# One attention-plus-two-block kernel: sums of weight columns formed once and kept in DRAM, output products in groups of two, GpSimd taken out of the second block

## The chip, the cores and the metric

One Trainium2 chip, one of its cores. The metric is the device time of the program in microseconds (us); lower is better. Engines are named as in the profile: PE is TensorE's matmul, PEld its weight load, DVE is VectorE, ACT is ScalarE, POOL is GpSimd, SP is SyncE (here it only issues DMAs).

## What is computed

Attention with a threshold mask (4 batches, 8 heads, 576 rows, 64 columns), whose output is reshaped to 2304 x 512, and then two feed-forward blocks. Only the second block bears on the change:

```python
x = _moe_ref(x, w_in, w_out, alpha)   # first block, d_ff = 2048
a = x @ w1                            # second block: 512 -> 1024
b = x @ w2
h = a * b @ w3                        # 1024 -> 1024
return h @ w_out                      # 1024 -> 512
```

All weights arrive as float64 (int64 words for the kernel) and are converted on the chip. Every matmul factor is cut in a high and a low part (`split_hi`, `split_lo`), and a product is three passes: high by high, high by low, low by high.

## The kernel before, in words

**Stages.** Attention runs to about 300 us of the trace. The first block follows, tile by tile in the order 0, 4, 1, 2, 3 (tile 4 holds 256 rows, the others 512). Then a stage multiplies w3 by the second w_out (`wp_job`), to about 757 us. Then the second block runs to 1052 us; it multiplies x by w1 and w2, multiplies the two results element by element, and multiplies that by the product of w3 and w_out.

**Order.** From the first block on, every instruction is an `Op` with a list of engines and an assumed cost on each. `list_order` (line 34) plays through these costs and fixes both the engine and the order in which each engine gets its instructions; on the chip each engine runs its list in that order and waits where a semaphore is not there yet. An op that lists "P" and "V" goes to POOL or DVE, whichever the planner expects to be earlier. `slots` gives how many buffers each tag has. PE's order in the second block is fixed by the order in which the code makes the ops (`pe`, line 1300).

**Second block.** 24 iterations: three passes (two halves of 384 rows each) by eight slices `f` of 128 columns. In an iteration `a` and `b` of both halves come from seven products of six 384-column matmuls each, instead of eight (a Strassen-Winograd scheme). The products J(1) to J(7) need sums and differences on three sides:

- of x, per pass: four differences (`difference`, tag `tt`, line 1170) and seven split tiles (tag `T`), in `moving`;
- of the weights, per iteration: four sums of 128 x 256 (line 1241, all on POOL), and four split tiles (tag `sw`, line 1262), in `stationary`. These tiles are made two iterations ahead;
- of the results: an ACT copy of the first two products (`c1`, `c11`, line 1380) and five DVE additions from PSUM (`u2`, `v5`, `c22`, `c12`, `c21`, line 1375).

Then `ab1` and `ab0` multiply a by b for either half (line 1375 too, as `ct<-ct`), ACT and DVE split the result (`x<-ct`, lines 183 and 188), and six output products `d` of three 512-column matmuls each (line 930 in this stage) are put in a queue that the next iteration empties, one `d` after each of six products (`d_next`). The products use two PSUM banks in turn, so a product waits until the bank's old value has been read: J(2) for `c1`, J(5) for `u2`, J(7) for `c11`, J(3) for `v5`, J(4) for `c22`, and the next iteration's first two for `c12` and `c21`. In the last iteration no `d` stands between the products.

**Where the weights come from.** While the first block runs, `put_by` loads slices of the later weights, converts them (`weight`: ACT, then three DVE steps, then a rounding add on POOL, line 218), and stores them in DRAM. `turns` says beside which step of the first block each conversion is planned: w1 and w2 first, then w_out, and w3 (which PE also transposes) during tile 2. In the second block `stationary` loads one slice of each of w1 and w2 per iteration.

Of the kernel before, what the change touches and what calls it, by code (L numbers as in the profile page):

```python
# [10 lines left out]
F32 = mybir.dt.float32  # L11
# [109 lines left out]
def kernel(  # L121
# [99 lines left out]
    with tc.manual_schedule():  # L221
# [565 lines left out]
        def weight(src, prio, after=()):  # L787
# [19 lines left out]
            ld = op({"S": 0.65}, load, prio - 12, take="raw")  # L807
# [41 lines left out]
        scratch = {}  # L849

        def put_by(key, src, prio, after, turned=False):
# [21 lines left out]

            s_ = op({"S": 0.65}, store, prio + (9 if turned else 4), [a])
# [4 lines left out]
        stored = {}  # L879

# [13 lines left out]
        def split(n, src, dst, prio, deps, take, free=(), psum=False):  # L894
            h = op(
                {"A": part(n, 0.48 if psum else 0.52)},
                lambda e: split_hi(ENG[e], dst()[:, 0, 0:n], src()),
                prio,
                deps,
                take=take,  # L900
            )
            l = op(
                {"V": part(n, 0.66 if psum else 0.6)},
                lambda e: split_lo(ENG[e], dst()[:, 1, 0:n], src(), dst()[:, 0, 0:n]),
                prio + 0.3,
                [h],
                free=free,
            )
            return h, l
# [149 lines left out]
        turns += [(t, f) for t in (1, 2) for f in sorted([3, 7, 11] + list(range(1, 14)))]  # L1059
# [95 lines left out]
        def moving(p, prio, deps_by_slot):  # L1155
# [11 lines left out]
            def temp():  # L1167
                return lazily(lambda: blk["pool"].tile([128, 2 * HT], F32, tag="tt", name="tt", bufs=3))

            def difference(dst, a, b, prio, deps):  # L1170
# [17 lines left out]
                return op({"P": 1.9, "V": 0.95}, emit, prio, deps, take="tt")  # L1188
# [15 lines left out]
            for i, (name, src, row, made) in enumerate(sources):  # L1204
# [11 lines left out]
                h = op({"A": 0.9}, lambda e, f=emit: f(e, False), prio + 1 + 0.5 * i, [made] if made else deps, take="T")  # L1216
                l = op({"V": 0.95, "P": 1.9}, lambda e, f=emit: f(e, True), prio + 1.3 + 0.5 * i, [h], free=[made] if made else [])
# [5 lines left out]
        def stationary(f, prio):  # L1223

            boxes, loads = [], []
            for i in range(2):
                x = lazily(lambda: dn.tile([128, 512], F32, tag="m", name="w12", bufs=3))

                def load(e, x=x, i=i):
                    nc.sync.dma_start(out=x(), in_=scratch[i, f])  # L1230

                boxes.append(x)
                loads.append(op({"S": 0.65}, load, prio - 8 + 0.1 * i, [stored[i, f]], take="m"))
            a, b = boxes
            sums = lazily(lambda: dn.tile([128, 1024], F32, tag="raw", name="sums"))
            lo2, hi2 = slice(0, 256), slice(256, 512)

            def tt(dst, x, y, how, prio, deps, take=None):
                o = op(
                    {"P": 0.74},  # L1240
                    lambda e: ENG[e].tensor_tensor(out=dst(), in0=x(), in1=y(), op=how),
                    prio, deps, take=take,
                )
                for d in deps:
                    if d in loads:
                        o.wait[d] = 2.6
                return o

            s1 = tt(lambda: sums()[:, lo2], lambda: b()[:, lo2], lambda: b()[:, hi2], ALU.add, prio - 3, [loads[1]], "raw")
            s3 = tt(lambda: b()[:, lo2], lambda: a()[:, lo2], lambda: b()[:, lo2], ALU.subtract, prio - 2.5, [s1, loads[0]])  # L1250
            s2 = tt(lambda: sums()[:, hi2], lambda: sums()[:, lo2], lambda: a()[:, lo2], ALU.subtract, prio - 2, [s1, loads[0]])
            s4 = tt(
                lambda: sums()[:, 512:768], lambda: a()[:, hi2], lambda: sums()[:, hi2], ALU.subtract, prio - 1.5, [s2]
            )
            parts, made = [], []
            for i, (src, deps, n, frees) in enumerate((
                (lambda: a(), [loads[0]], 512, [loads[0]]),
                (lambda: sums()[:, 0:512], [s1, s2], 512, []),
                (lambda: b(), [s3], 512, [loads[1]]),
                (lambda: sums()[:, 512:768], [s4], 256, [s1]),  # L1260
# [3 lines left out]
                    {"A": part(n, 0.52)}, lambda e, w=w, src=src, n=n: split_hi(ENG[e], w()[:, 0, 0:n], src()),  # L1264
                    prio + 0.5 * i, deps, take="wu0",
                )
                l = op(
                    {"P": part(n, 1.25), "V": part(n, 0.6)},
                    lambda e, w=w, src=src, n=n: split_lo(ENG[e], w()[:, 1, 0:n], src(), w()[:, 0, 0:n]),
                    prio + 0.5 * i + 0.3, [h], free=frees,  # L1270
                )
                for d in deps:
                    if d in loads:
                        h.wait[d] = 2.6
# [3 lines left out]
            for o in (s4,):  # L1278
                o.free.append(loads[0])
                loads[0].left += 1  # L1280
            made[1][1].free.append(s1)
            s1.left += 1
            s3.free.append(loads[0])
            loads[0].left += 1
# [212 lines left out]
```

## Time and profile before

| | us |
|---|---|
| median of three runs | 1058.74 (1057.98 to 1059.26) |
| the profiled execution | 1059.3 |
| its span, first to last instruction | 1057.5 |
| PE busy | 1021.9 (97%) |
| DVE busy | 767.4 (73%) |
| ACT busy | 575.9 (54%) |
| POOL busy | 486.5 (46%) |

A busy time adds up the recorded durations of an engine's instructions. Matmuls are pipelined, so a PE that is busy all the time is not necessarily at its best rate, and a wait of some tenths of a us shows as a gap between two of them. The time of an instruction on DVE or POOL as recorded includes any time in which it had begun and could not go on. Windows are counted in us from the first instruction.

### The profile page before, as it was taken

Reading aid. Unit: us, or ns where it says so; the run is one execution under the profiler, and the core shown is the slowest. Engines: PE = TensorE matmul, PEld = TensorE weight load, DVE = VectorE, ACT = ScalarE, POOL = GpSimd, SP = SyncE. Lnnn points to the kernel's source line nnn. Section 1 sums busy time; section 2 is a strip of 40 time slices with the busy share of each in tenths; the row PEclk is TensorE's granted clock in tenths of the full one; section 3 lists DMA queues with packets and bytes.
Section 4 is the critical chain, followed back from the end, with each engine's and each line's share of the span. In section 5 each row is a group of like instructions: output and inputs, shape, how many; then the busy total and the mean of one; then the engine's idle time right before and its main releaser. Section 6 shows DMA issues by size and latency. Waiting matters only on the chain.

```text
span 1057.5 us, 16956 instructions
## 1 busy us (share of the span) xinstructions
PE 1021.9 (97%) x5870; PEld 866.9 (82%) x5870; DVE 767.4 (73%) x1483; ACT 575.9 (54%) x1115; POOL 486.5 (46%) x609
## 2 busy tenths in 40 slices
PE   8999999999989999999999999999999989999997
PEld 6777787777758889988888888887888889888887
DVE  7999999999858886565566644358476796678663
ACT  5999989898866655545454432232333442344332
POOL 4888888888632332132212300024573463455320
PEclk9999999999999999999999999999999999999999
DMA  5353534344113333345534511103211121113101
GB/s 132 83 148 90 146 91 134 103 122 116 37 60 103 117 120 121 120 150 163 165 99 153 167 51 43 38 31 90 80 50 50 41 100 50 41 41 100 50 11 60
DMA packets 66837, 96.92 MB, mean 92 GB/s; under 512 B 14400, under 2 KB 43072, under 8 KB 66752
## 3 DMA queue, kind: packets, MB, share of 16 engines
q1 hardware_dynamic: 64544, 95.84, 30.6%
q8 instruction: 46, 0.75, 0.3%
q10 hardware_dynamic: 2208, 0.01, 0.1%
q14 instruction: 39, 0.32, 0.1%
HBM read 70.79 MB, written 15.20 MB: 81 GB/s over the span
## 4 chain that ended last, share of the span: by engine, by line
PE 79%; DVE 9%; POOL 5%; issue 3%; ACT 2%; DMA 1%; POOLq 0%; DVEq 0%; ACTq 0%
PE h L930 23%; PE acc L930 21%; PE h L1311 13%; PE pv_ps L518 8%; PE s_ps L402 5%; PE pt_ps L491 5%; DVE ct L1375 4%; POOL p L474 3%; PE tr L291 2%; DVE x L188 2%; POOL ks L181 1%; DVE tt L1184 1%; DVE T L188 1%; ACT ct L1380 1%; POOL qs L181 1%
## 5 line engine op out<-in xcount | busy, mean ns | idle before, releaser
L930 PE MATMUL h<-x,wa 128*128 128x512 f32 (+1 forms) x960 | 212.1, 370 | 1.2 <-ACT x L183 1.1
L1311 PE MATMUL h<-T,sw 128*128 128x384 f32 x1008 | 202.6, 341 | 9.8 <-DVE ct L1375 5.1
L930 PE MATMUL acc<-gs,wu 128*128 128x512 f32 (+1 forms) x960 | 209.6, 368 | 0.4 <-DVE wu L829 0.4
L1311 PEld LDWEIGHTS h<-T,sw 128*128 128x128 f32 x1008 | 179.9, 189 | 29.0 <-ACT ct L1380 11.3
L930 PEld LDWEIGHTS h<-x,wa 128*128 128x128 f32 x960 | 167.2, 189 | 32.2 <-ACT x L183 2.7
L930 PEld LDWEIGHTS acc<-gs,wu 128*128 128x128 f32 x960 | 168.2, 189 | 30.8 <-DVE wu L829 0.8
L218 POOL TENSOR_TENSOR m<-m,raw 128x512 int32<-128x512 int32 x58 | 81.4, 1403 | 230.2 <-DVE m L213 189.3
L426 DVE TENSOR_REDUCE sm<-s_ps 128x1 f32<-128x576 f32 x144 | 105.6, 752 | 12.9 <-PE s_ps L402 12.8
L437 ACT ACTIVATE e<-s_ps,sm 128x576 f32<-128x576 f32 x144 | 106.1, 765 | 7.4 <-DVE sm L426 4.7
L474 POOL TENSOR_SCALAR p<-p,sm 128x576 f32<-128x576 f32 x128 | 97.4, 767 | 27.1 <-DVE sm L467 18.1
L1375 DVE TENSOR_TENSOR ct<-h,ct 128x384 f32<-128x384 f32 x120 | 66.6, 555 | 50.7 <-PE h L1311 49.9
L451 DVE SCALAR_TENSOR_TENSOR p<-s_ps,sm,e 128x576 f32<-128x576 f32 x128 | 102.7, 812 | 0.9 <-ACT e L437 0.9
L1006 DVE SCALAR_TENSOR_TENSOR g<-h,salpha_sb,g 128x512 f32<-128x512 f32 (+1 forms) x80 | 55.6, 695 | 58.1 <-ACT g L1001 57.6
L491 PE MATMUL pt_ps<-ident,p 128*128 128x128 f32 x576 | 86.0, 276 | 11.6 <-ACT pt L505 8.8
L183 ACT CAST gs<-g 128x512 fp32r<-128x512 f32 (+1 forms) x80 | 46.3, 578 | 90.1 <-PE acc L930 71.9
L1001 ACT ACTIVATE g<-h,sign_sb 128x512 f32<-128x512 f32 (+1 forms) x80 | 51.3, 642 | 74.1 <-PE h L930 66.8
L183 ACT CAST x<-ct 128x384 fp32r<-128x384 f32 x48 | 24.7, 515 | 118.0 <-DVE ct L1375 117.9
L491 PEld LDWEIGHTS pt_ps<-ident,p 128*128 128x128 f32 x576 | 64.6, 140 | 26.7 <-POOL praw L474 10.4
L518 PE MATMUL pv_ps<-pt,vraw 128*64 128x256 f32 (+1 forms) x640 | 84.7, 411 | 0.4 <-ACT xT L531 0.2
L188 DVE TENSOR_TENSOR gs<-g,gs 128x512 fp32r<-128x512 f32 (+1 forms) x80 | 58.9, 737 | 34.0 <-ACT gs L183 33.5
L505 ACT COPY pt<-pt_ps 128x512 f32<-128x512 f32 x128 | 74.5, 597 | 15.6 <-PE pt_ps L491 14.6
L930 PE MATMUL acc<-wp,x 128*128 128x512 f32 x288 | 81.9, 395 | 0.3 <-DVE x L188 0.3
(127 smaller groups left out, 1709.4 us busy)
## 6 DMA issues: line engine op xcount, KB each, us to landing
raw<-in_moe_w_dram SPq DMA_DIRECT2D x32, 512.0 KB, 3.9
raw<-in_moe_w_out_dram SPq DMA_DIRECT2D x24, 512.0 KB, 3.5
w<-w SPq DMA_DIRECT2D x48, 256.0 KB, 2.6
qU<-qT SPq DMA_DIRECT2D x30, 320.0 KB, 4.1
wraw<-in_moe_w_in_dram SPq DMA_DIRECT2D x14, 512.0 KB, 3.7
w<-m SPq DMA_DIRECT2D x24, 256.0 KB, 2.2
z<-w SPq DMA_DIRECT2D x24, 256.0 KB, 2.7
qraw<-in_q_dram SPq DMA_DIRECT2D x16, 256.0 KB, 4.0
```

What stands on the lines that cost most here:

```text
L188: eng.tensor_tensor(out=dst, in0=src, in1=hi.bitcast(F32), op=ALU.subtract)
L218: nc.gpsimd.tensor_tensor(out=mc[0], in0=mc[0], in1=mc[1], op=ALU.add)
L426: nc.vector.tensor_reduce(out=sm_of(u, 0), in_=st[u], axis=AX.XY, op=ALU.max, negate=True)
L437: nc.scalar.activation(out=es[u].rearrange("p (j s) -> p j s", j=2), in_=st[u], func=AF.Exp, bias=sm_of(u, 0))
L451: nc.vector.scalar_tensor_tensor(out=p_at(u).rearrange("p (j s) -> p j s", j=2), in0=st.pop(u), scalar=sm_of(u, 1), in1=es.pop(u).rearrang ...
L474: nc.gpsimd.tensor_scalar(out=out, in0=in_, scalar1=sm_of(u, 3), scalar2=1.0, op0=ALU.mult, op1=ALU.mult)
L491: nc.tensor.transpose(t[:, i, :], p[:, at + i * 128 : at + (i + 1) * 128], ident)
L505: nc.scalar.copy(out=pt[:, g, 0:4, to], in_=ps)
L518: nc.tensor.matmul(out=o[64 * hh : 64 * hh + 64, 0:n], lhsT=vr[:, hh, i, :], rhs=pt[:, 0 if i == 4 and not half else hh, i, :], start=(i = ...
L930: nc.tensor.matmul(out=out, lhsT=l, rhs=r, start=first and i == 0, stop=last and i == n - 1)
L1311: nc.tensor.matmul(out=bank_()[:, 0:HT], lhsT=w()[:, ap_, kc * 128 : kc * 128 + 128], rhs=x()[:, bp, kc * HT : kc * HT + HT], start=first ...
L1375: lambda e: ENG[e].tensor_tensor(out=dst(), in0=x(), in1=y(), op=how),
```

## The change

- **Weight sums.** The four sums per slice move from `stationary` (POOL, 24 times four) to `put_sums`, called when w2's slice has been converted beside the first block (DVE, eight times four). Three tensors per slice are stored instead of two: w1's slice, the changed slice of w2, and the 768-column sums. `stationary` loads these three.
- **Order of conversions.** w_out now comes first, then w3 (tile 1 instead of tile 2), then w1 and w2 (tile 2 and the beginning of tile 3).
- **Engines.** In the second block all that could go to POOL or DVE goes to DVE: the differences, the low parts of `T` and `sw`, and the multiplications `ab0` and `ab1`. The planner's costs are new.
- **Output products.** Of the six `d`, two stand after J(6), two after J(5), one after J(3), one after J(4); before, one stood after each of J(6), J(2), J(5), J(7), J(3), J(4). In the last iteration four of them stand between the products.
- **Buffers.** `tt` has four buffers instead of three, `ct` six of 384 columns instead of eight (several results overwrite their inputs).
- **Stores.** The two 64-row stores of a tail group are one store.

```diff
@@ put_by @@
+            if key[0] == 1:
+                f = key[1]
+                made_12[key] = box, a
+                box_a, box_b, sums, s3, s4 = put_sums(f, prio + 4)
+                held = [first, first_of.pop((0, f)), box["ld"]]
...
+                    ("a", 512, lambda: box_a["x"], s4),
+                    ("b", 512, lambda: box_b["x"], s3),
+                    ("s", 768, lambda: sums()[:, 0:768], s4),
...
+                    outs.append(op({"S": 0.65}, put, prio + 6, [dep]))
+                o = op({"D": 0.0}, lambda e: None, prio + 6, outs, free=held)
...
+        def put_sums(f, prio):
...
+                return op(
+                    {"V": 0.43},
+                    lambda e: ENG[e].tensor_tensor(out=dst(), in0=x(), in1=y(), op=how),
+                    prio, deps,
+                )
+
+            A = lambda half: lambda: x_of(box_a)[:, half]
+            Bb = lambda half: lambda: x_of(box_b)[:, half]
+            s1 = tt(lambda: sums()[:, lo2], Bb(lo2), Bb(hi2), ALU.add, prio, [a, b])
+            s3 = tt(Bb(lo2), A(lo2), Bb(lo2), ALU.subtract, prio + 0.2, [s1])
+            s2 = tt(lambda: sums()[:, hi2], lambda: sums()[:, lo2], A(lo2), ALU.subtract, prio + 0.4, [s1])
+            s4 = tt(lambda: sums()[:, 512:768], A(hi2), lambda: sums()[:, hi2], ALU.subtract, prio + 0.6, [s2])
@@ the order of the conversions @@
-        later = [((i, f), cols(w, f)) for f in range(NF2) for i, w in enumerate((w1, w2))]
-        later += [(("o", j), rows(w_out2, j)) for j in range(NF2)]
+        later = [(("o", j), rows(w_out2, j)) for j in range(NF2)]
         later += [(("3", i, h), rows(w3, i, h)) for i in range(NF2) for h in range(2)]
+        later += [((i, f), cols(w, f)) for f in range(NF2) for i, w in enumerate((w1, w2))]
...
-        turns += [(t, f) for t in (1, 2) for f in sorted([3, 7, 11] + list(range(1, 14)))]
+        turns += [(1, f) for f in sorted([3, 7, 11] + list(range(1, 14)))]
+        turns += [(2 + f // NF, f % NF) for i in range(NF2) for f in (3 * i, 3 * i + 1)]
@@ moving @@
-                return op({"P": 1.9, "V": 0.95}, emit, prio, deps, take="tt")
+                o = op({"V": 1.0}, emit, prio, deps, take="tt")
+                o.bias = 0.3
+                return o
...
-                l = op({"V": 0.95, "P": 1.9}, lambda e, f=emit: f(e, True), prio + 1.3 + 0.5 * i, [h], free=[made] if made else [])
+                l = op({"V": 1.0}, lambda e, f=emit: f(e, True), prio + 1.3 + 0.5 * i, [h], free=[made] if made else [])
@@ stationary @@
-            for i in range(2):
+            for i, (what, n) in enumerate((("a", 512), ("s", 768), ("b", 512))):
...
-            s1 = tt(lambda: sums()[:, lo2], lambda: b()[:, lo2], lambda: b()[:, hi2], ALU.add, prio - 3, [loads[1]], "raw")
...
-                    {"P": part(n, 1.25), "V": part(n, 0.6)},
+                    {"V": 0.158 + n / 960},
                     lambda e, w=w, src=src, n=n: split_lo(ENG[e], w()[:, 1, 0:n], src(), w()[:, 0, 0:n]),
@@ the iteration @@
-            P_ = part(HT, 0.66)
+            P_ = 0.56
             q = now
-            n_d = 0 if end else 1
             j1 = J(1, bx, True, x_free, q)
...
-            d_next(q + 2.1, n_d)
+            d_next(q + 2.1, 2)
...
-            d_next(q + 3.8, n_d)
...
-            d_next(q + 5.5, n_d)
+            d_next(q + 5.5, 2)
...
-            d_next(q + 7.3, n_d)
...
-            d_next(q + 9.0, n_d)
+            d_next(q + 9.0, 1 if not end else 0)
...
-            d_next(q + 10.7, 99 if end else 1)
+            d_next(q + 10.7, 1 if not end else 99)
...
-            both = {"V": part(HT, 0.6), "P": part(HT, 1.25)}
-            ab1 = tt(t["c12"], t["c12"], t["c22"], ALU.mult, 0, q + 10.2, [c12, c22], free=[c22], engines=both)
-            ab0 = tt(t["c21"], t["c11"], t["c21"], ALU.mult, 0, q + 11.8, [c21, c11], free=[c11], engines=both)
+            ab1 = tt(t["c12"], t["c12"], t["v"], ALU.mult, 0.56, q + 9.7, [c12, c22], free=[v5])
+            ab0 = tt(t["u"], t["c11"], t["u"], ALU.mult, 0.56, q + 11.4, [c21, c11], free=[c11])
...
-                            for k_ in range(2):
-                                r0 = (2 * c + k_) * S + SM
-                                nc.sync.dma_start(out=out[r0 : r0 + ST, :], in_=out_()[64 * k_ : 64 * k_ + 64])
+                            dst = out.rearrange("(b s) d -> b s d", b=B)[2 * c : 2 * c + 2, SM:S, :]
+                            nc.sync.dma_start(out=dst, in_=out_())
...
-        slots = {"raw": 2, "m": 3, "u": 2, "gs": 2, "x": 4, "h": 4, "acc": 1, "wa": 16, "wu0": 8, "wu1": 8, "ct": 8, "tt": 3, "T": 7}
+        slots = {"raw": 2, "m": 3, "u": 2, "gs": 2, "x": 4, "h": 4, "acc": 1, "wa": 16, "wu0": 8, "wu1": 8, "ct": 6, "tt": 4, "T": 7}
```

## Rows read from the trace of the kernel before

**Rows 1.** Windows, tile 3 and second block: PE, PEld, DVE, ACT, POOL busy, clock, DMA
```profile
594.00:677.00 83.00, 83.00 (x377) 68.79 (x376) 41.72 (x68) 27.02 (x44) 5.78 (x4) 1.00 0.23 67
...
757.00:1052.20 295.20, 285.07 (x1442) 258.17 (x1440) 203.97 (x299) 111.24 (x225) 136.76 (x133) 0.99 0.17 52
```

**Rows 2.** What the seven products' matmuls and weight loads (line 1311) waited for: us, times
```profile
  ACT ct L1380: 16.0, 29
  DVE ct L1375: 11.6, 7
```

**Rows 3.** Chain of work that ended last, second block: start us, us, what
```profile
1022.98 1.06 PE h L1311 x6
1024.04 0.70 PE acc L930 x3
1024.74 2.10 PE h L1311 x12
...
1044.65 1.38 PE h L930 x6
```

**Rows 4.** Busy time by windows (columns of rows 1), each from one iteration's J(2) to a later one's
```profile
791.22:840.02 48.80, 47.47 (x242) 42.82 (x241) 31.90 (x50) 15.48 (x33) 19.29 (x20) 1.00 0.17 45
840.02:868.26 28.24, 25.38 (x120) 22.86 (x121) 26.55 (x34) 16.32 (x29) 20.62 (x16) 0.94 0.26 91
868.26:940.88 72.62, 70.76 (x361) 64.15 (x360) 47.97 (x74) 23.20 (x49) 28.70 (x30) 1.00 0.16 45
940.88:955.11 14.23, 11.99 (x60) 10.84 (x61) 13.22 (x20) 9.53 (x20) 9.92 (x9) 1.00 0.12 36
955.11:1027.38 72.27, 70.75 (x362) 64.25 (x361) 50.20 (x76) 25.98 (x53) 29.52 (x29) 1.00 0.19 59
```

**Rows 5.** Timeline, end of one iteration: start us, us, engine, instruction [idle before]
```profile
815.68 1.31 PE L1311 MATMUL h<-T,sw 128*128 128x384 f32 x6 [0.42 <-ACT ct L1380]
...
813.06 1.64 DVE L1375 TENSOR_TENSOR ct<-ct 128x384 f32<-128x384 f32 x1
814.62 0.42 DVE L188 TENSOR_TENSOR sw<-sums,sw 128x256 fp32r<-128x256 f32 x1
...
814.73 0.51 ACT L183 CAST x<-ct 128x384 fp32r<-128x384 f32 x1 [2.05 <-DVE ct L1375]
815.15 0.47 ACT L1380 COPY ct<-h 128x384 f32<-128x384 f32 x1
...
812.69 1.60 POOL L188 TENSOR_TENSOR sw<-w,sw 128x512 fp32r<-128x512 f32 x1
```

**Rows 6.** Timeline, the iteration after: one DVE and two POOL instructions
```profile
822.90 0.56 DVE L1375 TENSOR_TENSOR ct<-ct 128x384 f32<-128x384 f32 x1
...
822.28 0.74 POOL L1241 TENSOR_TENSOR w<-w,w 128x256 f32<-128x256 f32 x1
822.98 1.08 POOL L1241 TENSOR_TENSOR sums<-sums,w 128x256 f32<-128x256 f32 x1
```

**Rows 7.** Groups of instructions by line and shape, 757 to 1052.2 us
```profile
L1375 DVE TENSOR_TENSOR ct<-h,ct 128x384 f32<-128x384 f32 x120 | 66.6, 555 | 50.7 <-PE h L1311 49.9
L1375 DVE TENSOR_TENSOR ct<-ct 128x384 f32<-128x384 f32 x46 | 46.6, 1013 | 1.0
L188 DVE TENSOR_TENSOR T<-xT,T 128x768 fp32r<-128x768 f32 x2 | 1.9, 952 | 0.1
```

**Rows 8.** Instructions that touch the weight tiles: duration ns min/median/max, first, last start
```profile
L188 DVE TENSOR_TENSOR sw<-w,sw x29: 679/693/1777, 753.2 to 1026.2; 128x512 fp32r<-128x512 f32 x29
```

**Rows 9.** Timeline where a pass begins: a DVE difference, and a stall of PE
```profile
849.11 1.49 DVE L1184 TENSOR_TENSOR tt<-xT,tt 128x768 f32<-128x768 f32 x1
...
856.78 2.29 PE L1311 MATMUL h<-T,sw 128*128 128x384 f32 x6 [1.89 <-DVE ct L1375]
```

**Rows 10.** Timeline, issues of the half-size stores at the end
```profile
1050.09 2.44 SPq L1451 DMA_DIRECT2D out_dram<-o  x4
```

**Rows 11.** Costliest groups of instructions over the whole span (page): the rounding adds
```profile
L218 POOL TENSOR_TENSOR m<-m,raw 128x512 int32<-128x512 int32 x58 | 81.4, 1403 | 230.2 <-DVE m L213 189.3
```

More of the change, by code (lines that the diff above doesn't have):

```diff
@@ L805, in add @@
                 box["x"] = cvt_round((box["m"], box["c"]))
-            ld = op({"S": 0.65}, load, prio - 12, take="raw")
+            ld = box["ld"] = op({"S": 0.65}, load, prio - 12, take="raw")
             c = op({"A": 0.57}, low, prio, [ld] + after)
@@ L1167, in temp @@
             def temp():
-                return lazily(lambda: blk["pool"].tile([128, 2 * HT], F32, tag="tt", name="tt", bufs=3))
+                return lazily(lambda: blk["pool"].tile([128, 2 * HT], F32, tag="tt", name="tt", bufs=4))
             def difference(dst, a, b, prio, deps):
@@ L1250, in stationary, with load @@
[L1250 to L1254, printed above, removed]
-            parts, made = [], []
[L1256 to L1260, printed above, removed]
+            for i, (what, n) in enumerate((("a", 512), ("s", 768), ("b", 512))):
+                tag = "raw" if n > 512 else "m"
+                x = lazily(lambda n=n, tag=tag: dn.tile([128, 1024 if n > 512 else n], F32, tag=tag, name="w12", bufs=3 if tag == "m" else 2))
+                def load(e, x=x, what=what, n=n):
+                    nc.sync.dma_start(out=x()[:, 0:n], in_=scratch[what, f])
+                boxes.append(x)
+                loads.append(op({"S": 0.65}, load, prio - 8 + 0.1 * i, [stored["12", f]], take=tag))
@@ L1261, in stationary @@
+            a, sums, b = boxes
+            parts, made = [], []
+            for i, (src, ld, n, last) in enumerate((
+                (lambda: a(), loads[0], 512, True),
+                (lambda: sums()[:, 0:512], loads[1], 512, False),
+                (lambda: sums()[:, 512:768], loads[1], 256, True),
+                (lambda: b(), loads[2], 512, True),
             )):
@@ L1277, in stationary @@
                 made.append((h, l))
[L1278 to L1284, printed above, removed]
             def at(i, half):
                 return (lambda: parts[i]()[:, :, 256 * half : 256 * half + 256]), made[i]
-            return {1: at(0, 0), 2: at(0, 1), 3: at(3, 0), 4: at(2, 1), 5: at(1, 0), 6: at(1, 1), 7: at(2, 0)}, made
+            return {1: at(0, 0), 2: at(0, 1), 3: at(2, 0), 4: at(3, 1), 5: at(1, 0), 6: at(1, 1), 7: at(3, 0)}, made
         x_bank, y_bank = bank("h"), bank("h")
@@ L1321, in temp @@
         def temp():
-            return lazily(lambda: blk["pool"].tile([128, HT], F32, tag="ct", name="ct", bufs=8))
+            return lazily(lambda: blk["pool"].tile([128, HT], F32, tag="ct", name="ct", bufs=6))
         def d_piece(g, gs, f, first, last):
@@ L1359 @@
             made = S_made.pop(i)
-            t = {n: temp() for n in ("c1", "u2", "v5", "c11", "c22", "c12", "c21")}
+            t = {n: temp() for n in ("u", "v", "c11", "c12")}
             def J(k, bank_, first, deps, prio, s=s, m=m):
@@ L1401 @@
+            j5 = J(5, by, True, [u2], q + 4.5)
+            v5 = tt(t["v"], Y, t["u"], ALU.add, P_, q + 5.8, [j5, u2], take="ct")
+            d_next(q + 5.5, 2)
+            j7 = J(7, bx, True, [c11], q + 6.9)
+            c22 = tt(t["v"], X, t["v"], ALU.add, P_, q + 8.0, [j7, v5])
             j3 = J(3, by, False, [v5], q + 8.0)
-            c12 = tt(t["c12"], Y, t["u2"], ALU.add, P_, q + 9.3, [j3, u2], take="ct")
-            d_next(q + 9.0, n_d)
+            c12 = tt(t["c12"], Y, t["u"], ALU.add, P_, q + 9.1, [j3, u2], take="ct")
```

84 lines of the change are left out of this document (43 added, 41 removed).

## Prediction

> **What bounds the kernel now.** I read the busy windows first. From the first block's tile 3 on, PE has no gap: 83.00 of 83.00 us [rows 1]. In the second block it is busy 285.07 of 295.20 us, with DVE at 203.97 and POOL at 136.76 [rows 1]. So only the second block has something to give back, and the question is what PE waits for there. The waits of the products' line name ACT's copies out of PSUM (16.0 us in 29 waits, weight loads included) and DVE's additions (11.6 us in 7) [rows 2].
>
> Next comes the length of an iteration. The chain of waits gives the price of work without a stall: two products in a row 2.10 us, a lone product 1.06, a lone output product `d` 0.70 [rows 3]. The present pattern is one pair of products, five lone ones and six lone `d`: 2.10 + 5 x 1.06 + 6 x 0.70 = 11.60 us. The windows show what the iterations take [rows 4]: 48.80 us for four, 72.62 and 72.27 for six each, that is 2.40 + 3.02 + 2.67 = 8.1 us over the floor in 16 steady iterations (0.5 each). Where a new pass begins they show 28.24 us for two and 14.23 for one, 5.0 + 2.6 = 7.7 us over. Both together are 15.8 us.
>
> The steady stall has one cause, which the timeline shows [rows 5]. POOL begins a low part of `sw` at 812.69 and holds on for 1.60 us. DVE begins `ab0` at 813.06 and takes 1.64 us, ending at 814.70, when POOL has been done for about 0.4 us. The same multiplication took 0.56 us ten us later [rows 6], when POOL's own instruction, begun just after it, took 1.08 instead of 0.74 us: the two don't run together, the second waits. ACT has `x<-ct` at the head of its list, waiting for `ab0`; behind it stands the copy `c1`, at 815.15; and J(2), which waits for `c1`, starts 0.42 us late [rows 5]. Over the block the multiplications average 1013 ns, against 555 for the additions that read PSUM, which POOL does not disturb [rows 7].
>
> **The change, part by part.**
>
> *GpSimd out of the second block.* All of its 136.76 us of work go [rows 1]; the sums disappear, the rest comes to DVE. DVE's load then, at undisturbed durations: 120 additions at 0.555 (66.6 us), 48 multiplications and 48 low parts of x at 0.56 (53.8), 72 low parts of `sw` at 0.69 (49.7) [rows 6 to 8], 24 half-width ones at 0.42 (10.1) [rows 5], 14 low parts of `T` at 0.95 (13.3) [rows 7], eight differences at as much (7.6): 201 us, as now (203.97), because the lengthening goes. A steady iteration needs 7.5 of 11.5 us. `ab0` becomes 1.08 us shorter, more than the stall of 0.42, so the steady stall goes. What is late next is judged below. The 8.1 us are the gain; I keep back 0.1 us an iteration, 2.0 in all, for an urgent DVE instruction behind one of 0.56 to 0.95 us (bounds 0 and the present 8.1).
>
> *Groups of two.* The new pattern is three pairs of products (6.30), one lone (1.06), two pairs of `d` at 1.38 (2.76), two lone `d` (1.40): 11.52 us [rows 3]. That is 0.08 less, and over some 22 iterations 1.8 us. It moves covers too. J(2) gets 0.68 us more behind J(1), so this edit alone would also hide the 0.42 us stall. J(4) loses 0.70: between J(7) and J(4) stand J(3) and one `d`, 1.06 + 0.70 = 1.76 us, in which `c22` must run. It needs 0.56 and some 0.2 for two hops; an instruction of 0.95 in front of it still fits (1.71), two don't. The other covers stay as they are. In the last iteration four `d` move up between the products, and two are left to hide the chain `c12`, `ab1`, split high, split low (four times about 0.55, with hops 2.8 us) after J(3), against 1.06 + 1.38 = 2.44: I charge 0.5 us (bounds 0 and 1.5).
>
> *Beginning of a pass.* Here DVE is the engine that is late: it is busy 26.55 of 28.24 us [rows 4], and PE's stalls end with DVE additions (1.89 us before J(5), the longest) while differences run on DVE too, one of them for 1.49 us where a `T` of the same size takes 0.95 [rows 9, 7]. After the stall the products' group took 2.29 us instead of 1.06 [rows 9, 3], and the window's granted clock is 0.94, where the steady ones have 1.00 [rows 4]: part of the time ran at the lower of PE's two levels, 1.2 GHz instead of 2.4, and that part (1.2 us on this group alone) goes with the stall. With POOL's share on DVE, the two iterations need 2 x 7.5 + 7 x 0.95 + up to five differences (4.8) = 26.5 us, less 0.08 us of overlap between neighbours (814.62 starts before 813.06 + 1.64 [rows 5]) for some 40 instructions: 23.3 us, against 23.0 of PE. There is no margin if all differences fall there; with a fourth `tt` buffer the last difference of a pass need not wait for the pass before, and without any differences it is 18.9. So I keep back 2.0 us here and 0.5 at the second beginning, 2.5 of 7.7 (bounds 0 and 7.7).
>
> *Sums in the first block.* DVE gets 32 additions of 0.42 us, 13.4 us, in tile 2 and the beginning of tile 3; half-width, as the row taken for the price [rows 5]. They lie beside a PE without gaps, with DVE at 41.72 of 83 us in tile 3 [rows 1]; the bounds are 0 and 13.4, a gain is excluded since PE has nothing to give back there, and I take 0. New is the wait of the first sum on POOL's rounding add (1.40 us [rows 11]): behind it on DVE stand `prelu` and `split_lo` of the current step, and PE's `x2_job` waits for these; it is planned two and a half steps later, so several us are covered. The three steps of reordering (w_out, w3, then w1 and w2) move the same conversions; w3's transposes go to tile 1. The slots of tag `m` and `raw` are held until the stores have landed; the next pair is planned two steps on. SP issues 8 stores and 24 loads more on a queue that has no other work near its limit (DMA share 0.17 [rows 1]), and the `sw` tiles are made two iterations ahead: 0.
>
> *Stores at the end.* Two issues fewer of 0.61 us [rows 10] stand ahead of the last stores: 0.5 us (bounds 0 and 1.2).
>
> **Sum.** Gains 8.1 + 7.7 + 1.8 + 0.5 = 18.1 us; kept back 2.0 + 2.5 + 0.5 = 5.0; net 13.1. The profiled execution took 1059.3 us (span 1057.5, 1.8 around it), which gives 1046.2; against the median 1058.74 it is 1045.6 us. With nothing kept back it is 1040.6.
>
> **A rule on sharing work.** DVE is busy 69% of the second block and 94% of the windows where a pass begins [rows 1, 4]; that is the one fact that speaks against loading it. The Trainium skill, "Perfetto Trace Analysis", section "Optimizing Scalar/DVE Operations", says that with DVE saturated it may make sense to offload work even to GpSimd, though offloading between the two might not help since they share an SBUF read port. By the first half of that rule the change goes the wrong way, which is the rival A below; the pair of rows with 0.56 and 1.08 us is on the side of its second half.
>
> **The rivals.**
>
> *A. DVE becomes the bound where a pass begins.* All eleven `T` and `tt` instructions of a pass now stand in DVE's one list, and the planner starts whatever is ready, so an addition that PE waits for can stand behind two or three of them. For it: the 23.3 against 23.0 us above. Against it: the fourth buffer. Then none of the 7.7 us comes back: 18.1 - 7.7 - 2.0 - 0.5 = 7.9, 1050.8 us. It is the same if `c22` is late in every iteration by about 0.25 us.
>
> *B. Slower: DVE stalls in tiles 2 and 3.* Eight times DVE stands at the first sum for POOL's add (1.40 us) and then does four sums (1.7): 3.1 us in which no PSUM bank of the first block is read. If the cover of two and a half steps is not there, PE pays all of it, 24.8 us, and the time is 1070. It decides from 13.1 / 8 = 1.6 us per pair on. Against it: PE's full windows with DVE at half load [rows 1].
>
> *C. No change.* B at half its price takes what the second block gives: within 2.1 us of before.
>
> **How the numbers follow.** Forecast 0.69 (1040.6 to 1049), A 0.19 (1049 to 1055), C 0.05, B 0.07. The predicted time is the forecast's, 1045.6. The range goes from all gains at no cost, 1040.5, to the slow half of A's, 1054. About 0.2% (2.1 us) can be told from no change: faster 0.87, same 0.05, slower 0.08, the last with a little of C.
>
> **What would show it.** Right: POOL without instructions from about 757 us on; the `ct<-ct` group at 0.56 us instead of 1013 ns; steady iterations of 11.5 to 11.7 us; no granted clock below 1.00 where a pass begins. A shows as DVE additions ahead of a stalled J(5) or J(6) at the two beginnings, or of J(4) in every iteration. B shows as PE below 82 of 83 us in tiles 2 and 3, with DVE waiting for POOL's line 218. The prediction is wrong if multiplications stay long without POOL, if the block starts more than 3 us later than 757, or if the ends of the iterations wait for `sw` tiles.

## The result and the profile after

The changed kernel took 1048.7 us (1048.38 to 1049.04, four runs) where the kernel before took 1059.0 (1057.98 to 1061.17, four runs); the ratio is 0.990, interval 0.9883 to 0.9917. The forecast was 1045.6, with a range of 1040.5 to 1054. The time lies in it, but not by the terms given: the second block gained more than forecast, and the end of the kernel lost 8.9 us where half a us of gain was expected.

The busy windows of the changed kernel, columns as in rows 1 (the second one is the second block up to PE's last matmul):

```profile
594.00:677.00 83.00, 83.00 (x368) 68.73 (x367) 51.33 (x89) 34.34 (x57) 12.43 (x9) 1.00 0.39 135
757.00:1032.40 275.40, 275.36 (x1435) 255.61 (x1433) 179.35 (x338) 115.05 (x225) 0.00 (x0) 1.00 0.26 84
...
844.00:862.00 18.00, 18.00 (x95) 16.75 (x94) 14.72 (x28) 10.73 (x21) 0.00 (x0) 1.00 0.52 175
...
936.00:950.00 14.00, 14.00 (x76) 13.11 (x75) 11.23 (x21) 9.16 (x18) 0.00 (x0) 1.00 0.53 176
```

PE has no gap left in the second block, not even in the two windows where a pass begins (844 to 862, 936 to 950), with the granted clock at 1.00; POOL does nothing. Tile 3 of the first block stayed full, though DVE is busy 51.33 us in it instead of 41.72 [rows 1].

The groups of DVE, 757 to 1032.4 us, after (x, mean ns, as rows 7):

```profile
L1405 DVE TENSOR_TENSOR ct<-h,ct 128x384 f32<-128x384 f32 x120 | 66.9, 557 | 91.6 <-PE h L1341 91.4
L188 DVE TENSOR_TENSOR sw<-w,sw 128x512 fp32r<-128x512 f32 x69 | 45.8, 684 | 0.0
L1405 DVE TENSOR_TENSOR ct<-ct 128x384 f32<-128x384 f32 x48 | 26.7, 555 | 1.0
L188 DVE TENSOR_TENSOR x<-ct,x 128x384 fp32r<-128x384 f32 x48 | 26.4, 549 | 0.1
```

The multiplications take 555 ns instead of 1013 [rows 7]. DVE has all of POOL's work but the sums and is busy 179.35 us, less than the 203.97 before [rows 1]. I had counted 201 from single durations. All groups of this view add up to 194.2 us, and where two neighbours overlap (by up to some 0.08 us) a busy time counts the overlap once.

Pieces of the chain that ended last in the changed kernel (start us, us, what), as rows 3:

```profile
756.09 9.42 PE h L1341 x54
...
1014.79 1.06 PE h L1341 x6
1015.85 0.70 PE acc L985 x3
1016.55 2.10 PE h L1341 x12
...
1020.04 2.08 PE h L1341 x12
...
1026.64 2.30 PE acc L985 x9
...
1030.32 2.05 PE acc L985 x9
1032.37 0.02 issue
1032.39 0.59 ACT o L1467
```

All steps are PE's, and but for one they have the prices of rows 3: the three `d` at 1026.64, in the last iteration, take 2.30 us where the last three take 2.05. An iteration takes 11.50 us (778.2 to 789.7, with PE busy 11.50). The last matmul ends at 1032.37. The span is 1046.6. That leaves 14.2 us for an eviction and the last stores, which before took 5.3 us (1052.17 to 1057.5). The same chain in the kernel before:

```profile
757.27 5.27 PE h L1311 x30
...
1050.11 2.05 PE acc L930 x9
1052.17 0.02 issue
```

SP's own queue and the DMA share show where they go (timeline: start us, us; then windows after PE's end, columns as in rows 1):

```profile
1030.28 1.30 SPq L1476 DMA_DIRECT2D out_dram<-o  x2
1031.65 4.73 SPq L1473 DMA_DIRECT2D out_dram<-o  x3
```

```profile
1032.40:1036.00 3.60, 0.00 (x0) 0.00 (x0) 0.00 (x0) 0.58 (x1) 0.00 (x0) 1.00 0.20 48
1036.00:1038.00 2.00, 0.00 (x0) 0.00 (x0) 0.00 (x0) 0.00 (x0) 0.00 (x0) 0.73 0.98 326
1038.00:1040.00 2.00, 0.00 (x0) 0.00 (x0) 0.00 (x0) 0.00 (x0) 0.00 (x0) 0.50 0.30 104
1040.00:1046.60 6.60, 0.00 (x0) 0.00 (x0) 0.00 (x0) 0.00 (x0) 0.00 (x0) 0.50 0.10 40
```

Before, DMA worked at 0.91 to 0.94 in each us from 1052 to 1056, the last of them

```profile
1055.00:1056.00 1.00, 0.00 (x0) 0.00 (x0) 0.00 (x0) 0.00 (x0) 0.00 (x0) 0.50 0.94 361
```

The two merged stores are issued sooner than the four halves of rows 10 (1.30 us against 2.44). But then DMA works at a share of 0.20, for 2 us at 0.98 when the three last stores move, and at 0.10 for the rest (0.13 from 1040 to 1044, which would be two engines of 16). SP's issues of these last three take 4.73 us. The stores' time to landing, before and then after:

```profile
DMA to landing us min/median/max: 2.0/2.4/3.4
...
DMA to landing us min/median/max: 2.0/2.5/12.6
```

So by the traces: PE starts the second block 1.2 us earlier (756.09 instead of 757.27), runs it in 276.3 us instead of 294.9, and the tail takes 8.9 us more; 1.2 + 18.6 - 8.9 = 10.9 us, the difference of the spans.

### The profile page after: what moved, and what is told of

Same layout as the page of the kernel before. It is cut to its first block, busy times and chain, and to the rows that moved or that the text cites. A ratio compares the mean times of both kernels' runs of the same rounds, so it can differ in the third digit from the quotient of the medians.

```text
span 1046.6 us, 16928 instructions
## 1 busy us (share of the span) xinstructions
PE 1012.8 (97%) x5870; PEld 865.4 (83%) x5870; DVE 751.5 (72%) x1552; ACT 583.5 (56%) x1122; POOL 340.8 (33%) x469
## 4 chain that ended last, share of the span: by engine, by line
PE 87%; POOL 6%; DVE 2%; issue 2%; ACT 1%; DMA 1%; POOLq 0%; DVEq 0%; ACTq 0%
PE h L985 25%; PE acc L985 24%; PE h L1341 17%; PE pv_ps L518 8%; PE s_ps L402 5%; PE pt_ps L491 5%; POOL p L474 3%; PE tr L291 2%; POOL ks L181 1%; POOL qs L181 1%; PE zero L352 1%; PE h L858 1%; POOL praw L474 1%; DMA raw<-in_moe_w_dram 1%; DVE sm L426 0%
## 5 line engine op out<-in xcount | busy, mean ns | idle before, releaser
L1341 PE MATMUL h<-T,sw 128*128 128x384 f32 x1008 | 190.5, 335 | 0.0
L474 POOL TENSOR_SCALAR p<-p,sm 128x576 f32<-128x576 f32 x128 | 97.2, 767 | 26.6 <-DVE sm L467 17.6
L188 DVE TENSOR_TENSOR gs<-g,gs 128x512 fp32r<-128x512 f32 (+1 forms) x80 | 61.2, 765 | 46.5 <-ACT gs L183 45.8
L183 ACT CAST sw<-w 128x512 fp32r<-128x512 f32 (+1 forms) x96 | 54.0, 569 | 55.4 <-PE h L1341 53.6
```

The lines of the kernel that those rows point to most:

```text
L183: eng.copy(out=dst, in_=src)
L474: nc.gpsimd.tensor_scalar(out=out, in0=in_, scalar1=sm_of(u, 3), scalar2=1.0, op0=ALU.mult, op1=ALU.mult)
L1341: nc.tensor.matmul(out=bank_()[:, 0:HT], lhsT=w()[:, ap_, kc * 128 : kc * 128 + 128], rhs=x()[:, bp, kc * HT : kc * HT + HT], start=first ...
```

## Experiments

Each time stands with its ratio to the kernel before, as run beside it. The medians of the kernel before differ between these sets of runs (1059.0 to 1061.5 us), so a few tenths of a us between two sets say nothing.

### The merged store, both ways

**Changed kernel with the two half stores.**

```diff
-                            dst = out.rearrange("(b s) d -> b s d", b=B)[2 * c : 2 * c + 2, SM:S, :]
-                            nc.sync.dma_start(out=dst, in_=out_())
+                            for k_ in range(2):
+                                r0 = (2 * c + k_) * S + SM
+                                nc.sync.dma_start(out=out[r0 : r0 + ST, :], in_=out_()[64 * k_ : 64 * k_ + 64])
```

> The changed kernel with the two 64-row stores of a tail group put back. In the changed kernel PE ends at 1032.4 us of a span of 1046.6, 14.2 us before the end; before the change it ended 5.3 us before the end. Theory S (the single 128-row store is slow, and the last stores queue behind it): the end comes back to about 5.3 us after PE's last matmul, and the time falls by 8.9 us to 1039.5. Rival Q (the end is long because SP's list or the last iteration's new order is late): the tail stays near 14 us and the time near 1048.5.

1039.37 us (1039.12 to 1039.63), ratio 0.9797 (0.9783 to 0.9812). SP's queue at the end:

```profile
1029.88 2.45 SPq L1477 DMA_DIRECT2D out_dram<-o  x4
1032.43 1.51 SPq L1473 DMA_DIRECT2D out_dram<-o  x3
```

and the stores' time to landing:

```profile
DMA to landing us min/median/max: 2.0/2.4/4.2
```

The span is 1037.3, 9.3 us less; PE's last matmul ends at 1031.97, 5.3 us before the end, as in the kernel before. The last three issues are through in 1.51 us. Theory S holds; Q falls, since the last iteration's order is the changed one here too. This version beats both kernels, and none below is faster.

**Kernel before with the merged store.** The same edit the other way round.

> The kernel before with nothing changed but the two 64-row stores of a tail group made one store of [2, 64, 512]. Theory S: the span grows by about 9 us, to a time of 1068, with all of it after PE's last matmul. Rival Q: no change, 1059, or half a us less, as my forecast had it.

1068.52 us (1068.29 to 1069.67), ratio 1.0074 (1.0059 to 1.0089) to the 1061.03 beside it. Windows after PE's last matmul (1052.69):

```profile
1052.70:1056.00 3.30, 0.00 (x0) 0.00 (x0) 0.00 (x0) 0.58 (x1) 0.00 (x0) 0.86 0.15 39
1056.00:1058.00 2.00, 0.00 (x0) 0.00 (x0) 0.00 (x0) 0.00 (x0) 0.00 (x0) 0.50 0.91 292
1058.00:1060.00 2.00, 0.00 (x0) 0.00 (x0) 0.00 (x0) 0.00 (x0) 0.00 (x0) 0.50 0.45 150
1060.00:1066.90 6.90, 0.00 (x0) 0.00 (x0) 0.00 (x0) 0.00 (x0) 0.00 (x0) 0.50 0.11 41
```

The same picture as in the changed kernel: 14.2 us of tail, 10.2 us of it at a DMA share of 0.15 or less. The store alone makes the kernel before slower, by 7.5 us against this 1061.03.

**How many engines a store gets.**

```diff
-                            dst = out.rearrange("(b s) d -> b s d", b=B)[2 * c : 2 * c + 2, SM:S, :]
+                            dst = out.rearrange("(b s) d -> b s d", b=B)[:, SM + 32 * c : SM + 32 * c + 32, :]
```

> The changed kernel, its store of a tail group taking 32 rows of each of four batches ([4, 32, 512]) instead of 64 rows of each of two ([2, 64, 512]); as many bytes, as many rows, as many stores. The tail rows of the output are put in another order than the reference's. In the changed kernel the DMA share after the other stores are through is 0.13, which is 2 of 16 engines, at 50 GB/s. Theory E (a store is spread over as many engines as its outermost dimension has entries): the share in the tail becomes 0.25, the two stores take half as long, the end comes some 9 to 10 us after PE's last matmul instead of 14.2, and the time is about 1044. Rival H (any store of several runs of rows is slow by its shape, or the second store waits for the first): no change, 1048.5. The Trainium skill, page DMA: Bandwidth & Descriptors, section Rules for kernel authors, states the rule of theory E.

1044.08 us (1043.26 to 1045.07), ratio 0.984 (0.9827 to 0.9853). PE ends at 1033.76, the span at 1043.3: 9.5 us of tail. After the stores that overlap with others the window reads

```profile
1040.00:1042.00 2.00, 0.00 (x0) 0.00 (x0) 0.00 (x0) 0.00 (x0) 0.00 (x0) 0.50 0.22 85
```

In the changed kernel a window of the same length, with nothing but the two merged stores still moving, reads

```profile
1040.00:1042.00 2.00, 0.00 (x0) 0.00 (x0) 0.00 (x0) 0.00 (x0) 0.00 (x0) 0.50 0.13 51
```

That is 0.22 where two runs gave 0.13, and 85 GB/s where they gave 51. Both bytes and rows are the same, so H falls. With twice the entries in the outer dimension the share is nearly twice as large: E holds, as far as a share tells the number of engines. The stores with their 128 rows outermost, beside the merged ones, bring it to 0.98 (1036 to 1038 us of the changed kernel). The Trainium skill's page DMA: Bandwidth & Descriptors, section "Rules for kernel authors", has the rule that the slowest dimension sets the number of engines, so that an outermost size below 16 confines the whole DMA to at most that many. The two shares agree with it: 0.13 is 2.1 of 16 engines, 0.22 is 3.5.

### What removed the stalls

**Single output products in the changed kernel** (two half stores).

```diff
-            d_next(q + 2.1, 2)
+            d_next(q + 2.1, 0 if end else 1)
...
+            d_next(q + 3.8, 0 if end else 1)
...
-            d_next(q + 5.5, 2)
+            d_next(q + 5.5, 0 if end else 1)
...
+            d_next(q + 7.3, 0 if end else 1)
...
```

The planned times of J(2), J(7) and what reads them go back with this, and in the last iteration no `d` stands between the products, as before.

> The changed kernel with two stores, and with one output product after each of six products as before, instead of groups of two. Theory G (GpSimd's absence is what removes the steady stall, grouping only saves engine switches and cover): iterations of 11.6 us instead of 11.5, no stall, 1.8 us more than the kernel with two stores: 1041.3. Rival C (the longer cover of J(2) is needed): J(2) is late again by some tenths in each iteration, 0.3 to 0.5 us times 20, 1047 to 1051.

1041.7 us (1041.33 to 1042.36), ratio 0.9818 (0.9802 to 0.9834), 2.3 us over the kernel with groups. None of its matmuls waits; the group of the products (x, mean ns, idle before):

```profile
L1341 PE MATMUL h<-T,sw 128*128 128x384 f32 x1008 | 199.0, 338 | 0.0
```

Theory G holds, C falls: with POOL out, the longer cover of J(2) is not needed, and grouping is worth what the prices of rows 3 say (0.08 us an iteration) and some tenths, the other order of the last iteration included.

**Groups of two in the kernel before.**

```diff
-            d_next(q + 2.1, n_d)
+            d_next(q + 2.1, 2 * n_d)
...
-            d_next(q + 3.8, n_d)
...
-            d_next(q + 5.5, n_d)
+            d_next(q + 5.5, 2 * n_d)
...
-            d_next(q + 7.3, n_d)
```

> The kernel before with nothing changed but the places of the output products: groups of two in all iterations but the last, which stays as it was. The 0.68 us of cover that J(2) gains is more than its stall of 0.42, so by both theories the steady stall of J(2) goes; what tells them apart is whether GpSimd's work lengthens something else into a stall. Theory G: J(4), with 1.76 us of cover instead of 2.46, is now late when c22 stands behind a lengthened DVE instruction; of 8.1 + 1.8 us at most half comes, 1054; the beginnings of passes keep their 7.7 us. Rival C (grouping does it alone): all 9.9 us come, 1049.

1052.98 us (1052.42 to 1054.53), ratio 0.9928 (0.9912 to 0.9943): some 6 to 8 us less. The waits of the products (PE and weight loads; us, times), to be held against rows 2:

```profile
  DVE ct L1375: 15.9, 21
  ACT ct L1380: 2.8, 4
```

Most waits for ACT are gone, 2.8 us in 4 instead of 16.0 in 29. There are more waits for DVE. One kind the timeline of DVE and POOL shows (start us, us), with the chain's J(5) behind it:

```profile
802.98 1.65 DVE L188 TENSOR_TENSOR x<-ct,x 128x384 fp32r<-128x384 f32 x1
804.55 0.55 DVE L1375 TENSOR_TENSOR ct<-h,ct 128x384 f32<-128x384 f32 x1
...
802.73 1.48 POOL L188 TENSOR_TENSOR sw<-w,sw 128x512 fp32r<-128x512 f32 x1
...
805.15 1.32 PE h L1311 x6
```

A low part of x takes 1.65 us beside POOL, and `u2` stands behind that, so J(5) ends late: its piece takes 1.32 us instead of 1.05. I had named J(4) as the one that would be late; it is J(5). But this costs little: from 867.41 to 925.60, five iterations take 58.19 us, 0.6 over the price. The larger loss lies where the passes begin. There the chain goes mainly through DVE for some 20 us each time; pieces of it:

```profile
854.11 2.34 DVE tt L1184
...
942.91 4.36 DVE tt L1184 x3
...
952.03 2.37 PE h L1311 x12
```

Three iterations take 40.00 us at the first beginning (827.41 to 867.41) and 38.23 at the second (925.60 to 963.83), where the price of three is 34.56: 9.1 us over. So theory G held in its main points: a part of the gain came (1054 expected), and the beginnings kept their loss; rival C fell. The planner also gave POOL more work than before, 148.34 us between 757 and 1025 instead of 134.59, so that the places of `d` are not all that changed.

**The engines alone: POOL keeps only the sums** (kernel before; single products).

```diff
-                return op({"P": 1.9, "V": 0.95}, emit, prio, deps, take="tt")
+                return op({"V": 0.95}, emit, prio, deps, take="tt")
...
-                l = op({"V": 0.95, "P": 1.9}, lambda e, f=emit: f(e, True), prio + 1.3 + 0.5 * i, [h], free=[made] if made else [])
+                l = op({"V": 0.95}, lambda e, f=emit: f(e, True), prio + 1.3 + 0.5 * i, [h], free=[made] if made else [])
...
-                    {"P": part(n, 1.25), "V": part(n, 0.6)},
+                    {"V": 0.158 + n / 960},
...
-            both = {"V": part(HT, 0.6), "P": part(HT, 1.25)}
+            both = {"V": 0.56}
```

> The kernel before with low parts, differences and multiplications of the second block on DVE alone, as in the change; the four weight sums stay on POOL in the second block, output products stand singly, and nothing else is changed. POOL then works 4 x 0.74 = 3.0 us of each iteration instead of 5 to 8. Theory P (every POOL instruction makes a DVE instruction with two SBUF inputs wait, whatever it computes): multiplications average 0.6 to 0.8 us, J(2) is late by 0.1 to 0.2 us in part of the iterations, the beginnings of passes keep 2 to 4 us; time 1044 to 1049. Rival L (only POOL's long low parts of 1.6 us do harm): as the changed kernel with two stores and single products, 1041 to 1043.

1042.35 us (1041.73 to 1043.3), ratio 0.9837 (0.9823 to 0.9851). The group of the multiplications:

```profile
L1375 DVE TENSOR_TENSOR ct<-ct 128x384 f32<-128x384 f32 x48 | 31.9, 664 | 1.0
```

Theory P falls as to the time: POOL is busy 76.8 us between 757 and 1025, the multiplications average 664 ns, and still the products wait for DVE only 2.2 us in 5. These four `{"V": ...}` bring some four fifths of what the changed kernel with half stores gains (1.6% of 2.0%). Two of them also change an assumed cost, and so perhaps the order of DVE's list; that was not tried apart. L holds as to the time: POOL's sums, 0.80 to 0.95 us on average here, lengthen DVE's work, but by less than the covers hold. That the long low parts alone do the harm is not shown by this run; the run with POOL allowed again bears on it.

**The same with groups of two.** This is the changed kernel with half stores and without the move of the sums, but for the buffers, the order of the conversions and the last iteration, which stay as before. To the edit above it adds:

```diff
-            d_next(q + 2.1, n_d)
+            d_next(q + 2.1, 2 * n_d)
...
-            d_next(q + 3.8, n_d)
...
-            d_next(q + 5.5, n_d)
+            d_next(q + 5.5, 2 * n_d)
...
-            d_next(q + 7.3, n_d)
```

> The kernel before with low parts, differences and multiplications on DVE alone and with groups of two, the weight sums still on POOL in the second block; two stores. It is the changed kernel with two stores without its move of the sums. If the sums' move is worth next to nothing, as the kernel with the sums alone on POOL and single products said (1042.35 against 1041.7): 1039.4 to 1040.5. Rival: with the groups J(4)'s cover is 0.70 us shorter, and a multiplication or addition behind a POOL sum makes it late: 1042 to 1045.

1040.11 us (1039.77 to 1040.81), ratio 0.9803 (0.979 to 0.9816), against 0.9797 (0.9783 to 0.9812) with the sums in DRAM. Forming the sums once is worth about 0.7 us by both pairs of medians (2.0 and 0.6 by the ratios), and the intervals of the ratios do not tell it from nothing.

**POOL allowed again in the changed kernel** (half stores; sums out of the block).

```diff
-                    {"V": 0.158 + n / 960},
+                    {"P": part(n, 1.25), "V": 0.158 + n / 960},
...
+            both = {"V": 0.56, "P": part(HT, 1.25)}
-            ab1 = tt(t["c12"], t["c12"], t["v"], ALU.mult, 0.56, q + 9.7, [c12, c22], free=[v5])
+            ab1 = tt(t["c12"], t["c12"], t["v"], ALU.mult, 0, q + 9.7, [c12, c22], free=[v5], engines=both)
```

(and the same for `ab0`, for the low parts of `T` and for the differences)

> The changed kernel with two stores, in which the planner may again give low parts of T and sw, differences and multiplications to POOL or DVE at the costs it had before; sums stay out of the block and products stay in groups of two. Theory P: POOL gets work again, DVE's instructions with two SBUF inputs become longer by what POOL still has to do (multiplications 0.7 to 0.9 us on average), and some products wait again: 1043 to 1048. Rival N (with the sums gone and J(2)'s longer cover it does not matter who does the rest): 1039 to 1041.

1041.82 us (1041.24 to 1042.68), ratio 0.9832 (0.9818 to 0.9845): 2.4 us more than without POOL by the medians, less than theory P's lower end of 1043 and more than N's upper end of 1041. POOL works 97.2 us of the 268 between 757 and 1025, and DVE's multiplications are as long as before, yet only 3.9 us of waits come back. The group of DVE's multiplications, and what the products waited for (us, times):

```profile
L1405 DVE TENSOR_TENSOR ct<-ct 128x384 f32<-128x384 f32 x27 | 27.5, 1020 | 1.0
```

```profile
  DVE ct L1405: 3.9, 6
```

Neither theory is right as put. In the steady iterations PE has no gap, though DVE's multiplications are long; its gaps sit in the first iteration and at the first beginning of a pass (1.03 us at 855, the longest).

Together with two runs above this shows something else. The windows from 757 to 1025 us (columns as in rows 1), of the kernel before with only the sums on POOL (single products), of the kernel before with groups, and of this one:

```profile
757.00:1025.00 268.00, 267.60 (x1388) 248.24 (x1387) 192.76 (x333) 106.79 (x217) 76.82 (x91) 1.00 0.17 55
...
757.00:1025.00 268.00, 261.53 (x1342) 237.93 (x1341) 206.16 (x276) 105.66 (x214) 148.34 (x139) 1.00 0.18 56
...
757.00:1025.00 268.00, 266.61 (x1389) 247.27 (x1388) 184.79 (x248) 108.31 (x215) 97.22 (x82) 1.00 0.28 86
```

PE stands for 0.4 us with the sums alone on POOL, for 6.5 with the sums and the long instructions, and for 1.4 with the long instructions and without the sums. So POOL's work has no price by the piece: with groups of two and half stores the sums alone cost about 0.7 us, the long instructions alone 2.4, both together 13.6 (1052.98 against 1039.37). The kernel of the second window differs from this one also in the buffers, the planner's costs and the last iteration, so how much of the difference is the sums' is not shown.

### The rest

**Three `tt` buffers** (half stores).

```diff
-            return lazily(lambda: blk["pool"].tile([128, 2 * HT], F32, tag="tt", name="tt", bufs=4))
+            return lazily(lambda: blk["pool"].tile([128, 2 * HT], F32, tag="tt", name="tt", bufs=3))
...
-        slots = {"raw": 2, "m": 3, "u": 2, "gs": 2, "x": 4, "h": 4, "acc": 1, "wa": 16, "wu0": 8, "wu1": 8, "ct": 6, "tt": 4, "T": 7}
+        slots = {"raw": 2, "m": 3, "u": 2, "gs": 2, "x": 4, "h": 4, "acc": 1, "wa": 16, "wu0": 8, "wu1": 8, "ct": 6, "tt": 3, "T": 7}
```

> The changed kernel with two stores and three tt buffers, as before, instead of four. Theory F (as the forecast argued, the fourth buffer keeps a difference away from the beginning of a pass): 2 to 4 us of stall come back at the two beginnings, 1041.5 to 1043.5. Rival U (an undisturbed DVE has room there anyway): no change, 1039.4 within 1 us.

1039.37 us (1038.96 to 1039.5), no change. F falls: the fourth buffer was no reason for anything.

**Groups of three** (half stores).

```diff
-            d_next(q + 2.1, 2)
+            d_next(q + 2.1, 3)
...
-            d_next(q + 5.5, 2)
+            d_next(q + 5.5, 3)
...
-            d_next(q + 9.0, 1 if not end else 0)
...
-            d_next(q + 10.7, 1 if not end else 99)
+            d_next(q + 10.7, 0 if not end else 99)
```

> The changed kernel with two stores and output products in two groups of three, behind J(6) and J(5), so that J(7), J(3), J(4) and the next J(1), J(6) stand in a row. If every change between the two kinds of work costs 0.02 to 0.04 us on PE, iterations become 11.45 instead of 11.52 us and the time falls by 1 to 2 us, to 1038. Rival W: J(4), J(1) and J(6) have one product of 1.06 us as cover, c22, c12 and c21 need 0.56 and two hops, and any DVE instruction in front of them makes them late, 0.3 to 0.6 us per iteration: 1045 to 1050.

1041.3 us (1040.96 to 1042.05), ratio 0.9815 (0.9801 to 0.9828), about 2 us more. Neither came as put. The iterations don't stall, so W falls, and they gain next to nothing (11.49 us from one pair of products to the next). About half of the loss is at the end, where no `d` of the iteration before is left to hide the last chain:

```profile
1027.09 0.57 DVE ct L1405
...
1027.68 0.57 DVE ct L1405
...
1028.27 0.52 ACT x L183
...
1029.36 0.48 DVE x L188
```

That is the chain whose 2.8 us the prediction had set against 2.44 us of cover; here PE waits for it after its last product, 0.74 and 0.32 us. The rest of the 2 us was not traced.

**Half stores from two queues.**

```diff
-                                nc.sync.dma_start(out=out[r0 : r0 + ST, :], in_=out_()[64 * k_ : 64 * k_ + 64])
+                                (nc.sync, nc.scalar)[k_].dma_start(out=out[r0 : r0 + ST, :], in_=out_()[64 * k_ : 64 * k_ + 64])
```

> The changed kernel with two 64-row stores per tail group, the second of them issued from ACT instead of SP. SP issues the four half stores in 2.45 us and the last three in 1.51, and the last issue comes about 0.9 us after the last eviction. Theory I (SP's issuing holds up the end): 0.5 to 0.9 us less than with two stores on SP, 1038.6. Rival D (the transfers themselves, 1.5 MB, hold up the end, or ACT's evictions now wait behind its issues): no change or up to 0.6 us more, 1039.4 to 1040.

1039.38 us (1038.63 to 1039.65), no change, as D has it. The timeline shows D's second case at work (start us, us; q marks issues):

```profile
1031.40 0.50 ACTq L1477 DMA_DIRECT2D out_dram<-o  x1
1031.94 1.56 ACT L1467 COPY o<-acc 128x512 f32<-128x512 f32 x3 [0.57 <-PE acc L985]
```

ACT's last three evictions start when its own issue is through, and end at 1033.50 us instead of 1032.57. SP's last issue then ends at 1033.88, against 1033.94 with both halves on SP. So this run did not bring the last issue forward, and whether the half us that the prediction hoped for from two issues fewer is there to be had stays open.

## Why the prediction was right or wrong, point by point

**What bounds the kernel: right.** PE's gaps of the second block were all there was to gain in it, and they went. The price list of rows 3 gave 18.1 - 0.5 = 17.6 us for the block; it gave 18.6.

**GpSimd out of the block: mechanism right, the share of each part open.** The multiplications came down to 555 ns as the row at 822.90 [rows 6] had promised, and the kernel before with nothing but this edit on the engines, the sums left on POOL, took 1042.35 us. What I did not see is that POOL's instructions have no price by the piece: the sums alone, 76.8 us of POOL time, cost about 0.7 us, the long instructions alone 2.4, both together 13.6. Rows 5 show one meeting, a low part of 1.6 us beside `ab0`, which made the stall in that iteration.

**What was kept back: the terms mis-sized.** The 0.1 us an iteration and the 2.5 us at the beginnings of passes measured 0: PE has no gap between 757 and 1032 us. The 0.5 us at the last chain measured some 0.2, hidden in the 2.30 us of the three `d` at 1026.64, where a weight load waits 0.4 us for the low part of x. The chain was counted too long: its hops, put at some 0.1 us each and more, are 0.02 to 0.04 us in the chain of the run with groups of three. The argument for the beginnings, DVE's 23.3 us against PE's 23.0, counted five differences in that stretch by their place in the trace of before. After, only three short ones (1.09 us together, at 859.54) stand between 844 and 862, and DVE is busy 14.72 of 18.00 us in that window. The fourth buffer, which I gave as the reason, has no part in it. Rival A did not occur. The rule that it leaned on, the Trainium skill's "Optimizing Scalar/DVE Operations" in "Perfetto Trace Analysis", did not pay here in its first half (that with DVE saturated offloading may make sense): with POOL's share taken over, the sums aside, DVE was less busy, 179.35 us for 203.97.

**Groups of two: right in size, and not needed for the stall.** 1.8 us forecast, 2.3 us measured against single products. J(4)'s shorter cover held. As I wrote, grouping alone hides most of J(2)'s stall; what is left then (1052.98 us) sits mainly where the passes begin, 9.1 us, and J(5) is some 0.3 us late now and then.

**Sums in the first block: right.** The price was 0 and PE is full in tiles 2 and 3; the block starts 1.2 us earlier than before, which I had not counted (PE's windows show 0.8 of it: gaps of 0.66 us between 511 and 594 and of 0.64 between 677 and 757 are gone, and one of 0.48 between 428 and 511 is new; the rest was not traced). Rivals B and C did not occur. The gain that the move brings to the second block, which I had not priced apart, is about 0.7 us beside a POOL that does nothing else, and not told from nothing.

**Stores at the end: the step that failed.** It was forecast as 0.5 us gained, with bounds of 0 and 1.2, from SP's issues alone. It cost 8.9 us. My bounds looked only at the issue and left out that the transfer gets another shape; no row of before shows a store whose outermost dimension is two, and I should have bounded it on the side of a loss. The rule of the Trainium skill's page DMA: Bandwidth & Descriptors named above speaks of just this, and the prediction did not weigh it. The 0.5 us for the issues themselves stays open.

**The sum.** Forecast 13.1 us, by the spans 10.9. The error of 2.2 us is made of four: -9.4 at the stores, +5.0 kept back for nothing, +1.0 in the block, +1.2 before it. The range held by compensation, which is luck. Without the merged store the time was 1039.4, just below its lower end.

## What to carry to other kernels

A DVE multiplication of two SBUF inputs took 0.56 us here and 1.64 beside a POOL instruction of 1.60 us [rows 5, 6]. So what DVE is relieved of by POOL must be held against what POOL's instructions add to DVE's urgent ones. That price is not a sum over the pieces: taking the low parts, differences and multiplications from POOL and leaving it the sums was worth some 17 us, and taking the sums as well about 1 or less; but in the changed kernel, with the sums gone and groups of two, giving the rest back to POOL cost 2.4. A DMA that is merged to save an issue should keep its rows outermost: two entries outermost held the DMA share at 0.13 here, four at 0.22. The last stores of a kernel, which nothing hides, are the place to look at that first. An edit that looks like tidying deserves its own row or its own run before it is priced at nothing.

## What was not expected of the hardware

Two stores of [2, 64, 512], 256 KB each, moved at a DMA share of 0.13 when they were alone (1040 to 1044 us), and the slowest store took 12.6 us to land, against at most 4.2 us in the same kernel with stores of half the size; with four entries outermost the share was 0.22 and the slowest took 7.9 us. The issues behind them were held up too: SP took 4.73 us for the last three instead of 1.51.
